# Batch 0's last expert as a slot of 7 + 7 products, its weights made in spaced steps through batch 0

## The chip, the cores and the metric

One NeuronCore of a Trainium2 chip runs the whole program. The metric is the device time of one execution in microseconds (us). Five engines work side by side, each through its own queue in program order: TensorE (PE; its weight loads are PEld), VectorE (DVE), ScalarE (ACT), GpSimd (POOL) and SyncE (SP), which issues nearly all DMA transfers. An instruction at the head of a queue that waits holds everything behind it in that queue.

## The reference, cut to what matters

```python
def reference(q, k, v, centroids, w_gate, w1, w2):      # 4 batches, 8 heads, 768 tokens, head dim 64
    x = clustered_attention(q, k, v, centroids)         # tokens x 512, all batches in one: 3072 x 512
    P = exp(x @ w_gate - max); 8 rounds of row and column normalizing    # 3072 x 8
    out = 0
    for e in range(8):                                  # 8 experts, w1[e] 512 x 1024, w2[e] 1024 x 512
        h = maximum(x @ w1[e], 0)
        out += P[:, e:e+1] * (h @ w2[e])
```

Everything is float32. The kernel keeps each float32 factor as a pair of float16 numbers (high and low) and adds three matmuls, so a product of blocks is 3 matmuls for every 128 of the inner dimension.

## The kernel before, in words

The attention comes first (about 490 us). The experts follow: batch 0 in one way, batches 1 to 3 in another.

**Layer 1** (`layer1`, with `product`) is the same everywhere. For a quarter of an expert's hidden features (256 of 1024, `f2`) it computes h = x w1 by a 2 x 2 block scheme with seven products instead of eight. A product is six matmuls of 128 x 384. Order of the seven: B11 into the accumulator `pa`; S2 x T2 into `pb`; then A12 onto `pa`, S3 onto `pb`, S1 into a new `pa`, A22 onto `pb`, S4 onto the second `pa`. ACT copies the first one (`m1`, L1379) and the third (L1617). DVE reads the others in L1370: `u2` after product 1, `u3` after 3, then the results called `c` after products 4, 5 and 6. `h_ps` has two buffers. So the `pb` of the next quarter's second product takes the buffer that DVE's last `c` of this quarter reads.

**Batch 0** runs 32 quarters (t = 0 to 31: expert t // 4, quarter t % 4). Step m = 0 to 6 of quarter t holds one product of layer 1 and, for m > 0, one token tile of the layer 2 of quarter t - 1 (`layer2`): six matmuls of 128 x 512 into `o_ps`, all eight block products. In between stand, written out by hand and kept in that order on every engine by `plan.keep_order`, the steps of generators:

- `make_w`: while quarter t runs, the float16 pairs of the weights of quarter t + 1 are made from `raw` (a float32 load, 8 buffers): ACT scales (L1482), POOL forms four sums (`s1w`, L336) and the low halves (L1487, L1494), ACT the high halves, DVE the low halves of the second matrix (`wb`, L1472, two instructions).
- `scan`: two ACT instructions per quarter (`total`, L302) measure the size of the weights of a later quarter (t + 5); after an expert's fourth quarter `spread_powers` turns the figure into the expert's scale. It is a chain over two DMAs: DVE `am` (L1456), DMA `amw` to memory, DMA `all` back to every partition, seven small DVE instructions that begin with `gmax` (L1302) and end with `so` (L273). An expert's fourth scan stands in quarters t = 6, 10, 14, 18, 22 and 26. The scan's generator advances at m in `ANY`, five times per quarter.
- `next_x`: from t = 9 on the same kind of chain for the inputs of batch 1 (`amx`).
- `store_w`: SP writes the made weights to memory for the later batches (`w1d`, `w2d`: four DMAs per quarter).
- `layer2`'s `done`: in quarters t % 4 == 0 the finished expert is added to `acc` by DVE (L1555, six instructions of 128 x 512); expert 0's is copied by ACT (L1552) and later gated (`gate_first`, L1564).

`second_left` makes, at the end of batch 0, the sums of w2 of expert 0 that the seven-product layer 2 needs.

**Batches 1 to 3** run 24 slots, one per batch and expert. A slot has 28 steps: one product of layer 1 (L1356) and nine matmuls of 128 x 256 of the layer 2 of the slot before (`layer2b`, L1814: seven products, 252 matmuls), with the weights loaded as made. In the first slot layer 1 stands alone. `evict` (L1789) adds finished products to the four blocks C11, C12, C21, C22 and X. During batch 1 the sums of w2 of experts 1 to 7 are made (`second_sums` and what follows it).

## Time and profile before

| | |
|---|---|
| median of 3 runs | 2289.27 us (2289.05 to 2291.24) |
| the profiled execution's own time | 2289.5 us |
| its span, first to last instruction | 2287.7 us |
| PE busy | 2257.7 us, 99% |
| DVE busy | 1637.3 us, 72% |
| POOL busy | 1145.9 us, 50% |
| ACT busy | 1113.2 us, 49% |
| mean granted clock of TensorE | 0.998 |
| share of PE in the chain that ended last | 92% |

The span is what the trace sees; the execution's own time has 1.8 us more around it. "Busy" of PE is pipelined: one matmul's shown duration overlaps the next one's, so the pace of PE is read from the distance of starts. A quarter's place in time is read from the starts of its first product, and T below is that start.

### The profile page before, as it was taken

The numbers are of one execution on the slowest core, as the hardware profiler recorded it, in microseconds if no ns is written. First come the engines' busy times: TensorE is split into PE (matmuls) and PEld (weight loads), VectorE is DVE, ScalarE is ACT, GpSimd is POOL, SyncE is SP. The second block draws the span as 40 slices with busy tenths as digits, with TensorE's granted clock in tenths as the row PEclk, the third lists the DMA queues.
The fourth block names the chain that finished last, engine by engine and source line by source line (L and its number), as shares of the span: only waits on it lengthen the run. The fifth ranks groups of instructions, "written<-read, shape, count | busy, mean of one in ns | idle before, by whom it ended". The sixth has DMA issues, their size and how long they took to land.

```text
span 2287.7 us, 39676 instructions
## 1 busy us (share of the span) xinstructions
PE 2257.7 (99%) x15491; PEld 1523.3 (67%) x15491; DVE 1637.3 (72%) x2691; ACT 1113.2 (49%) x2048; POOL 1145.9 (50%) x1009
## 2 busy tenths in 40 slices
...
GB/s 173 120 125 162 168 157 159 118 167 239 196 150 170 195 158 131 221 262 212 211 233 219 226 222 177 169 128 152 151 159 137 187 169 133 129 132 137 143 116 102
DMA packets 226828, 383.93 MB, mean 168 GB/s; under 512 B 73408, under 2 KB 154640, under 8 KB 226128
## 3 DMA queue, kind: packets, MB, share of 16 engines
...
q14 instruction: 67, 0.55, 0.1%
...
## 4 chain that ended last, share of the span: by engine, by line
PE 92%; DVE 3%; DMA 2%; ACT 1%; POOL 1%; issue 1%; SPq 0%; ACTq 0%; DVEq 0%; POOLq 0%
PE h_ps L1356 37%; PE pb L1814 12%; PE pc L1814 8%; PE pa L1814 8%; PE av_ps L978 5%; PE o_ps L1540 3%; PE o_ps L1542 3%; PE o_ps L1541 3%; PE max_ps L835 3%; PE exp_ps L923 3%; PE exp_ps L924 2%; PE misc_ps L636 1%; PE misc_ps L1020 1%; POOL psum L945 1%; DVE mrt L839 1%
## 5 line engine op out<-in xcount | busy, mean ns | idle before, releaser
L1356 PEld LDWEIGHTS <-wa 128*128 128x128 f16 x5376 | 525.7, 98 | 300.0 <-issue 2.1
L1814 PEld LDWEIGHTS <-ho 128*128 128x128 f16 x6048 | 591.4, 98 | 139.7 <-DVE ho L1708 2.5
L1356 PE MATMUL h_ps<-xsT,wa 128*128 128x384 f16 x3072 | 581.6, 326 | 0.3 <-DVE u L1370 0.2
L1699 POOL TENSOR_TENSOR B<-B,B 128x768 f32<-128x768 f32 x96 | 196.5, 2049 | 488.2 <-DVE ho L1708 468.0
L1356 PE MATMUL h_ps<-xsB,wa 128*128 128x384 f16 x2304 | 436.7, 326 | 0.3 <-ACT m L1379 0.3
L1708 DVE TENSOR_TENSOR ho<-B,ho 128x768 f16<-128x768 f32 x288 | 350.2, 1217 | 0.1
L1370 DVE SCALAR_TENSOR_TENSOR u<-h_ps,m 128x384 f32<-128x384 f32 x256 | 141.7, 554 | 271.1 <-PE h_ps L1356 267.0
L1854 ACT ACTIVATE B<-B 128x384 f32<-128x384 f32 x288 | 149.7, 520 | 378.8 <-DVE B L1370 375.4
L1814 PE MATMUL pb<-w2o,ho 128*128 128x256 f16 x2592 | 328.7, 273 | 0.4 <-DVE ho L1708 0.4
L1704 ACT CAST ho<-B 128x768 f16<-128x768 f32 x288 | 230.3, 825 | 11.2 <-POOL B L1699 7.8
L839 DVE TENSOR_REDUCE mrt<-max_ps 128x1 f32<-128x512 f32 (+1 forms) x288 | 190.5, 685 | 54.3 <-PE max_ps L835 52.7
L945 POOL TENSOR_TENSOR psum<-psum,pe 128x512 f32<-128x512 f32 x160 | 208.0, 1318 | 35.0 <-ACT pe L930 28.1
L1814 PE MATMUL pa<-w2o,ho 128*128 128x256 f16 x1728 | 219.2, 273 | 1.2 <-DVE ho L1708 1.2
L1814 PE MATMUL pc<-w2o,ho 128*128 128x256 f16 x1728 | 219.2, 273 | 0.2 <-DVE ho L1708 0.2
L1699 POOL TENSOR_TENSOR B<-B,T 128x768 f32<-128x768 f32 x48 | 94.6, 1973 | 230.0 <-DVE ho L1708 207.7
L930 ACT ACTIVATE pe<-exp_ps 128x512 f32<-128x512 f32 x288 | 166.9, 598 | 51.2 <-PE exp_ps L924 39.5
L1379 ACT ACTIVATE m<-h_ps 128x384 f32<-128x384 f32 x128 | 62.6, 489 | 191.0 <-PE h_ps L1356 187.2
L1852 ACT ACTIVATE B<-h_ps 128x384 f32<-128x384 f32 x96 | 47.1, 490 | 203.3 <-PE h_ps L1356 203.3
L1542 PE MATMUL o_ps<-wb,hl 128*128 128x512 f16 x384 | 145.5, 379 | 0.0
L1541 PE MATMUL o_ps<-wb,hh 128*128 128x512 f16 x384 | 145.5, 379 | 0.0
L1540 PE MATMUL o_ps<-wb,hh 128*128 128x512 f16 x384 | 145.5, 379 | 0.0
L1370 DVE SCALAR_TENSOR_TENSOR B<-h_ps,u 128x384 f32<-128x384 f32 x192 | 105.9, 552 | 48.3 <-PE h_ps L1356 48.2
...
## 6 DMA issues: line engine op xcount, KB each, us to landing
...
```

The source lines that it names most:

```text
L839: nc.vector.tensor_reduce(out=t["mr"][:, i0 : i0 + ni, ni - 1], in_=ps.rearrange("p (x c) -> p x c", x=ni), axis=AX, op=ALU.max)
L930: nc.scalar.activation(pe, ps.rearrange("p (x c) -> p x c", x=ni), AF.Exp, scale=SCALE)
L945: (nc.gpsimd if e == POOL else nc.vector).tensor_tensor(out=st[:, o : o + N0], in0=old[o], in1=part, op=ALU.add)
L1356: nc.tensor.matmul(ps[:, 0:HB], wa[:, w_, a, c, :], x[:, x_, c, :], start=(first and s_ == 0), stop=(s_ == len(steps) - 1), skip_group_che ...
L1370: nc.vector.scalar_tensor_tensor(out=t, in0=ps[:, 0:HB], scalar=KAPPA, in1=x, op0=ALU.mult, op1=ALU.add)
L1540: nc.tensor.matmul(po[i], hh[:, t, ti], wbh[:, t], start=(first and t == 0), stop=False)
L1541: nc.tensor.matmul(po[i], hh[:, t, ti], wbl[:, t], start=False, stop=False)
L1542: nc.tensor.matmul(po[i], hl[:, t, ti], wbh[:, t], start=False, stop=(last and t == 1))
L1699: nc.gpsimd.tensor_tensor(out=t, in0=d[a], in1=d[c], op=ALU.subtract)
L1704: nc.scalar.copy(t[:, 0], blocks[n, g][o])
L1708: nc.vector.tensor_tensor(out=t[:, 1], in0=blocks[n, g][o], in1=t[:, 0], op=ALU.subtract)
L1814: nc.tensor.matmul(ps[:, q], h[:, h_, f, q * P : (q + 1) * P], w[:, 2 * g + f, w_], start=(first and g == 0 and s_ == 0 and q % 2 == 0), s ...
```

## The change

Batch 0 runs 28 quarters (`N1`) instead of 32. Its expert 7 becomes the first slot, ahead of those of batch 1: layer 1 alone in that slot, layer 2 by seven products in the next. The four blocks C11 to C22 are what batch 0 adds into (in place of `acc`), and stay for the slot; `done` writes 128 x 256 twice where it wrote 128 x 512 once, and the outputs leave from the slot.

The weights of expert 7 are made in batch 0 by steps ("chores") at fixed places: a step stands at the end of step m of quarter t where 7 t + m is its number. `last_scan` loads each of the eight halves (256 KB) and lets ACT measure it in place (t = 3 to 7); `last_scale` forms the scale (t = 7 to 9); `last_first` and `last_second` load each quarter of each matrix again and make it, one of four quarters of the expert every four quarters from t = 9 to t = 26. Their buffers take 15 KB per partition; `raw` has 7 buffers instead of 8 and loads six quarters ahead instead of seven. Expert 0's sums of w2 are made in batch 1 like those of 1 to 6, and `second_left` is gone. In quarters t % 4 == 2 the scan's generator advances at all seven steps, not five.

The diff, cut to its core:

```diff
-        rawp = pool("rawp", 8, ax)
-        accp = pool("accp", 1, ax)
+        rawp = pool("rawp", 7, ax)
+        lastp = pool("lastp", 1, ax)
...
-        def second_left(f2):
...
+        chores = {}
+
+        def spaced(gen, first, offsets):
+            for o in offsets:
+                chores.setdefault(first + o, []).append(gen)
+
+        def load_last(m, f2):
+            t = lastp.tile([P, 1024], F32, name="lr", bufs=2)
...
+        def last_first(f2):
+            raw = load_last(0, f2)
...
+            yield
+            nc.scalar.activation(raw, raw, AF.Copy, scale=s1[:, E - 1 : E])
+            yield
...
+            quads = ((slice(A22, A22 + 1), A[:, 0, 1:2]), (slice(A11, A12 + 1), A[:, 1]))
+            for o, a in quads:
+                nc.scalar.copy(y[:, 0, o], a)
+            sums(S_, A[:, 1, 0], A[:, 1, 1], A[:, 0, 0], A[:, 0, 1], nc.gpsimd)
+            yield
+            for o, a in quads:
+                nc.gpsimd.tensor_tensor(out=y[:, 1, o], in0=a, in1=y[:, 0, o], op=ALU.subtract)
+            yield
+            nc.sync.dma_start(out=d[:, :, A22 : A12 + 1], in_=y)
+            yield
+            y = raw.bitcast(F16).rearrange("p (x o c f) -> p x o c f", x=2, o=4, c=KC)
+            nc.scalar.copy(y[:, 0], S_)
+            yield
+            for o in (0, 2):
+                nc.gpsimd.tensor_tensor(out=y[:, 1, o : o + 2], in0=S_[:, o : o + 2], in1=y[:, 0, o : o + 2], op=ALU.subtract)
+            yield
+            nc.sync.dma_start(out=d[:, :, S1 : S4 + 1], in_=y)
+            yield
+
+        FIRST_AT = (1, 7, 12, 13, 16, 19, 20, 24)
+
+        def last_second(f2):
+            raw = load_last(1, f2)
...
+            for o, a in quads:
+                nc.scalar.activation(y[:, o, 0], a, AF.Copy, scale=scale)
+            yield
+            for o, a in quads:
+                nc.vector.scalar_tensor_tensor(out=y[:, o, 1], in0=a, scalar=scale, in1=y[:, o, 0], op0=ALU.mult, op1=ALU.subtract)
+            yield
...
+            sums(S_, r2[:, 1, 0:HD], r2[:, 0, 0:HD], r2[:, 1, HD:DO], r2[:, 0, HD:DO], nc.gpsimd)
...
+        SECOND_AT = (1, 7, 10, 12, 14, 19, 22, 25)
+
+        def last_scan(f2, m, am):
+            t = load_last(m, f2)
+            yield
+            total(am[:, m, f2 : f2 + 1], t, t)
+            yield
...
+        for f2 in range(NP2):
+            for m in range(2):
+                spaced(last_scan(f2, m, am_last), 7 * (3 + f2), (1 + 3 * m, 7 + 3 * m))
+            spaced(last_first(f2), 7 * (3 + 6 + 4 * f2), FIRST_AT)
+            spaced(last_second(f2), 7 * (3 + 8 + 4 * f2), SECOND_AT)
+        spaced(last_scale(am_last), 7 * (3 + 4), (5, 8, 11, 14))
...
-                    nc.vector.scalar_tensor_tensor(out=acc[:, i], in0=ps, scalar=gate, in1=acc[:, i], op0=ALU.mult, op1=ALU.add)
...
+                        else:
+                            nc.vector.scalar_tensor_tensor(out=t, in0=s_, scalar=gates_[:, i : i + 1], in1=t, op0=ALU.mult, op1=ALU.add)
...
-        AHEAD = 7
+        AHEAD = 6
...
-        for t in range(NI):
+        for t in range(N1):
...
-                if m in ANY:
+                if m in ANY or t % NP2 == 2:
                     step(scanning)
...
-                if t == NI - 1:
-                    step_left(m)
+                for x in chores.pop(7 * t + m, ()):
+                    step(x)
...
-    slots = [(b, e) for b in range(1, B) for e in range(E)]
+    slots = [(0, E - 1)] + [(b, e) for b in range(1, B) for e in range(E)]
...
-        if b == 1 and n:
+        if b == 1 and e < E - 1:
             first = base - SLOT
```

Where instructions moved, at three places. The first is DVE in quarter t = 6, the fourth quarter of the scan of expert 2 (t = 10, 14, 18 and 22 read alike). `gmax2` to `so` are the seven instructions that need the DMA `all2`; `c <- h_ps, u2` is the last result of the quarter. Before:

```order
L1370 SCALAR_TENSOR_TENSOR c_7297<-h_ps_7198,m1_7193 128x384
L1623 SCALAR_TENSOR_TENSOR hl_7185<-c_7277,hh_7184 128x384
L1472 SCALAR_TENSOR_TENSOR wb_7183<-raw_6539,s2_99,wb_7183 128x512
L1370 SCALAR_TENSOR_TENSOR c_7317<-h_ps_7270,u2_7205 128x384
L1623 SCALAR_TENSOR_TENSOR hl_7185<-c_7297,hh_7184 128x384
L1623 SCALAR_TENSOR_TENSOR hl_7185<-c_7317,hh_7184 128x384
L1302 TENSOR_REDUCE gmax2_7345<-all2_7301 128x2
L1303 TENSOR_SCALAR gmax2_7345<-gmax2_7345 128x2
```

After:

```order
L1370 SCALAR_TENSOR_TENSOR c_7335<-h_ps_7225,m1_7219 128x384
L1701 SCALAR_TENSOR_TENSOR hl_7211<-c_7312,hh_7210 128x384
L1302 TENSOR_REDUCE gmax2_7339<-all2_7293 128x2
L1303 TENSOR_SCALAR gmax2_7339<-gmax2_7339 128x2
L1304 TENSOR_SCALAR gmax2_7339<-gmax2_7339 128x2
L270 TENSOR_SCALAR ginv_7343<-gmax2_7339 128x2
L271 RECIPROCAL s1_98<-ginv_7343 128x1
L272 RECIPROCAL s2_99<-ginv_7343 128x1
L273 TENSOR_SCALAR so_100<-ginv_7343 128x1
L1476 SCALAR_TENSOR_TENSOR wb_7209<-raw_6546,s2_99,wb_7209 128x512
L1370 SCALAR_TENSOR_TENSOR c_7363<-h_ps_7305,u2_7232 128x384
```

The seven instructions moved from behind the quarter's last `c` and its two `hl` to a place ahead of the second `wb` and of that `c`.

The second is SP in the same quarter: the stores of the weights (`w1d5`, `w1d6` and their `w2d`), the pair `amw2`, `all2`, the loads `raw`, and after the change the loads `lr` of the chores. Before:

```order
L1529 DMA w1d5_109<-wa_6861 128x3584
L1531 DMA w2d1_6221<-wb_6862 128x2x256 x3
L1442 DMA raw_7179<-in_moe_w1 128x4x256
L1443 DMA raw_7179<-in_moe_w2 128x2x512
```

After, from the stores of quarter 5 on:

```order
L1607 DMA w1d5_109<-wa_6869 128x3584
L1609 DMA w2d1_6221<-wb_6870 128x2x256 x3
L1517 DMA lr_7163<-in_moe_w2 128x2x512
L1446 DMA raw_7205<-in_moe_w1 128x4x256
L1447 DMA raw_7205<-in_moe_w2 128x2x512
L1515 DMA lr_7253<-in_moe_w1 128x4x256
L1607 DMA w1d6_110<-wa_7045 128x3584
L1609 DMA w2d1_6221<-wb_7046 128x2x256 x3
L1295 DMA amw2_7270<-am2_7268 128x2
L1298 DMA all2_7293<-amw2_7270 128x256
L1517 DMA lr_7327<-in_moe_w2 128x2x512
```

A load `lr` stands ahead of quarter 6's stores; there are two `lr` buffers, so it waits until ACT has measured the one before the last.

The third is DVE in quarter t = 12, where expert 2 is finished (t = 16, 20 and 24 read alike): `acc` (after: C11 to C22) from `o_ps`. Before:

```order
L1370 SCALAR_TENSOR_TENSOR u3_8128<-h_ps_8074,m1_8069 128x384
L1623 SCALAR_TENSOR_TENSOR hl_8061<-c_8106,hh_8060 128x384
L1555 SCALAR_TENSOR_TENSOR acc_6310<-o_ps_7701,gates_8053,acc_6310 128x512
L1370 SCALAR_TENSOR_TENSOR c_8146<-h_ps_8139,u3_8128 128x384
L1472 SCALAR_TENSOR_TENSOR wb_8059<-raw_7179,s2_99,wb_8059 128x512
L1555 SCALAR_TENSOR_TENSOR acc_6310<-o_ps_7722,gates_8053,acc_6310 128x512
```

After:

```order
L1370 SCALAR_TENSOR_TENSOR u3_8214<-h_ps_8158,m1_8149 128x384
L1701 SCALAR_TENSOR_TENSOR hl_8141<-c_8191,hh_8140 128x384
L1636 SCALAR_TENSOR_TENSOR C11_6314<-o_ps_7764,gates_8133,C11_6314 128x256
L1636 SCALAR_TENSOR_TENSOR C21_6317<-o_ps_7764,gates_8133,C21_6317 128x256
L1567 SCALAR_TENSOR_TENSOR lq_8154<-lr_8031,s2_99,lq_8154 128x256 x3
L1370 SCALAR_TENSOR_TENSOR c_8237<-h_ps_8230,u3_8214 128x384
L1476 SCALAR_TENSOR_TENSOR wb_8139<-raw_7375,s2_99,wb_8139 128x512
L1636 SCALAR_TENSOR_TENSOR C22_6315<-o_ps_7785,gates_8133,C22_6315 128x256
L1636 SCALAR_TENSOR_TENSOR C12_6316<-o_ps_7785,gates_8133,C12_6316 128x256
```

Each addition became two, and three instructions of a chore stand ahead of the fifth product's `c`.

## Rows read from the trace of the kernel before

**Rows 1.** Busy time by stretch: columns us, PE, PEld, DVE, ACT, POOL (count), clock, DMA share, GB/s.

```profile
839.57:897.95 58.38, 58.38 (x313) 30.53 (x312) 39.66 (x62) 35.29 (x58) 31.36 (x32) 1.00 0.37 125
1156.71:1211.53 54.82, 54.82 (x423) 41.10 (x421) 48.16 (x68) 26.76 (x41) 34.64 (x25) 1.00 0.67 233
```

**Rows 2.** Timeline of PE, quarter 12: start us, us, instruction, count [idle before <-releaser].

```profile
664.09 1.14 PE L1356 MATMUL h_ps<-xsB,wa 128*128 128x384 f16 x6
...
678.68 1.14 PE L1356 MATMUL h_ps<-xsB,wa 128*128 128x384 f16 x6
679.66 1.14 PE L1356 MATMUL h_ps<-xsT,wa 128*128 128x384 f16 x6
```

**Rows 3.** Timeline of DVE, end of quarter 10 and into 11.

```profile
647.48 1.64 DVE L1472 SCALAR_TENSOR_TENSOR wb<-raw,s,wb 128x512 f16<-128x512 f32 x1
649.04 0.55 DVE L1370 SCALAR_TENSOR_TENSOR c<-h_ps,u 128x384 f32<-128x384 f32 x1
...
650.66 0.41 DVE L1302 TENSOR_REDUCE gmax<-all 128x2 f32<-128x256 f32 x1
...
651.97 0.55 DVE L1370 SCALAR_TENSOR_TENSOR u<-h_ps,m 128x384 f32<-128x384 f32 x1
```

**Rows 4.** Timeline of ACT, start of quarter 10.

```profile
636.46 1.05 ACT L302 ACTIVATE junk<-raw 128x1024 f16<-128x1024 f32 x1
...
637.50 1.14 ACT L1482 ACTIVATE raw<-raw,s 128x1024 f32<-128x1024 f32 x1
```

**Rows 5.** Timeline of SP's DMA issues, quarter 10.

```profile
642.96 0.33 SPq L1295 DMA_DIRECT2D amw<-am  x1
645.77 0.33 SPq L1298 DMA_DIRECT2D all<-amw  x1
```

**Rows 6.** Timeline of SP's DMA issues, quarters 13 and 14.

```profile
686.74 0.33 SPq L1295 DMA_DIRECT2D amx<-am  x1
687.13 0.43 SPq L1442 DMA_DIRECT2D raw<-in_moe_w  x1
...
695.37 0.34 SPq L1298 DMA_DIRECT2D all<-amx  x1
...
696.28 1.75 SPq L1531 DMA_DIRECT2D w2d<-wb  x3
701.34 0.33 SPq L1295 DMA_DIRECT2D amw<-am  x1
706.98 0.33 SPq L1298 DMA_DIRECT2D all<-amw  x1
```

**Rows 7.** Timeline of DVE, quarter 15.

```profile
711.82 0.42 DVE L1302 TENSOR_REDUCE gmax<-all 128x2 f32<-128x256 f32 x1 [2.70 <-DMA all<-amw]
```

**Rows 8.** Timeline of PE, quarter 15.

```profile
713.17 0.38 PE L1542 MATMUL o_ps<-wb,hl 128*128 128x512 f16 x1
713.74 1.14 PE L1356 MATMUL h_ps<-xsT,wa 128*128 128x384 f16 x6 [0.18 <-DVE u L1370]
```

**Rows 9.** Timeline of DVE, quarter 12.

```profile
673.52 0.74 DVE L1472 SCALAR_TENSOR_TENSOR wb<-raw,s,wb 128x512 f16<-128x512 f32 x1
674.35 0.75 DVE L1555 SCALAR_TENSOR_TENSOR acc<-o_ps,gates,acc 128x512 f32<-128x512 f32 x1
675.32 0.56 DVE L1370 SCALAR_TENSOR_TENSOR c<-h_ps,m 128x384 f32<-128x384 f32 x1 [0.22 <-PE h_ps L1356]
...
676.67 1.64 DVE L1472 SCALAR_TENSOR_TENSOR wb<-raw,s,wb 128x512 f16<-128x512 f32 x1
678.24 0.74 DVE L1555 SCALAR_TENSOR_TENSOR acc<-o_ps,gates,acc 128x512 f32<-128x512 f32 x1
678.90 0.54 DVE L1370 SCALAR_TENSOR_TENSOR c<-h_ps,u 128x384 f32<-128x384 f32 x1
```

**Rows 10.** Timeline of POOL, quarter 12.

```profile
675.18 2.59 POOL L1494 TENSOR_TENSOR wa<-s1w,wa 128x512 f16<-128x512 f32 x2 [2.11 <-ACT wa L1492]
```

**Rows 11.** The instructions of line L1789: count, min/median/max ns, first and last start, forms.

```profile
L1789 DVE SCALAR_TENSOR_TENSOR C<-pb,gates,C x195: 467/475/485, 1031.6 to 2238.3; 128x256 f32<-128x256 f32 x195
```

More of the change, by code (lines that the diff above doesn't have):

```diff
@@ L1508, in second_left @@
             sums(S_, r2[:, 1, 0:HD], r2[:, 0, 0:HD], r2[:, 1, HD:DO], r2[:, 0, HD:DO], nc.gpsimd)
             yield
-            y = t[:, 0:1024].bitcast(F16).rearrange("p (o x m) -> p o x m", o=4, x=2)
-            nc.scalar.activation(y[:, :, 0], S_, AF.Copy, scale=s2[:, 0:1])
+            nc.sync.dma_start(out=w2d[E - 1][:, A22 : A12 + 1, f2], in_=y)
             yield
-            nc.vector.scalar_tensor_tensor(out=y[:, :, 1], in0=S_, scalar=s2[:, 0:1], in1=y[:, :, 0], op0=ALU.mult, op1=ALU.subtract)
+            y = raw.bitcast(F16).rearrange("p (o x m) -> p o x m", o=4, x=2)
@@ L1514, in second_left @@
+            nc.scalar.activation(y[:, :, 0], S_, AF.Copy, scale=scale)
             yield
-            nc.sync.dma_start(out=w2d[0][:, 3:7, f2], in_=y)
+            nc.vector.scalar_tensor_tensor(out=y[:, :, 1], in0=S_, scalar=scale, in1=y[:, :, 0], op0=ALU.mult, op1=ALU.subtract)
             yield
-        LEFT_AT = ((0, 3, 4, 6), (1, 5, 6, 8), (2, 7, 8, 10), (3, 9, 10, 12))
-        def step_left(now):
-            for x, times in zip(lefting, LEFT_AT):
-                if now in times:
-                    step(x)
+            nc.sync.dma_start(out=w2d[E - 1][:, S1 : S4 + 1, f2], in_=y)
@@ new lines, in last_second, with last_scale @@
+            yield
[4 more added lines that the diff above has]
+            total(am[:, m, f2 : f2 + 1], t, t)
+            yield
+        def last_scale(am):
+            am2 = gs.tile([P, 2], F32, name="am2z", bufs=1)
+            nc.vector.tensor_reduce(out=am2, in_=am, axis=AX, op=ALU.max)
+            yield from spread_powers(am2, 2, f"amw{E - 1}", lambda g: weight_use(E - 1, g, gs))
+        am_last = gs.tile([P, 2, NP2], F32, name="am8z", bufs=1)
@@ L1563, in gate_first @@
             for i in range(NT):
-                nc.scalar.activation(acc[:, i], acc[:, i], AF.Copy, scale=gates_[:, i : i + 1])
+                j, q_ = divmod(i, NT // 2)
+                for name, (r, j_) in PARTS.items():
+                    if j_ == j:
+                        t = acc[name][:, q_]
+                        nc.scalar.activation(t, t, AF.Copy, scale=gates_[:, i : i + 1])
                 yield
-        AHEAD = 7
+        AHEAD = 6
         RIDES = ((0, 6), (1, 1)) + tuple((t, m) for t in (2, 3, 4, 5) for m in (2, 6))
@@ L1579, in attn_moe_kernel @@
         plan.unpin()
-        acc = accp.tile([P, NT, DO], F32, name="acc")
-        lefting = []
+        acc = {name: accb.tile([P, NT // 2, HD], F32, name=name) for name in PARTS}
         gating = iter(())
-        scans = {i - 5: (i,) for i in range(8, NI)}
-        loads = {0: (), 1: (4, 5), 2: (6, 7, 8), 3: (9, 10)}
+        scans = {i - 5: (i,) for i in range(8, N1)}
+        loads = {0: (), 1: (4, 5), 2: (6, 7, 8), 3: (9,)}
         loaded = {}
-        for t in range(NI):
+        for t in range(N1):
             e, f2 = divmod(t, NP2)
```

70 lines of the change are left out of this document (41 added, 29 removed).

## The prediction

> **What bounds the kernel now.** I looked first at the shares of busy time: PE is busy for 99% of the span at a granted clock of 0.998, so a change pays only by taking matmuls away, and costs only where it makes PE wait. Then the busy time by stretch: an expert of batch 0 in steady state (quarters 24 to 27) takes 58.38 us of PE with 313 matmul records, a slot of the later batches 54.82 us with 423 [rows 1]. PE is full in both, so the two lengths are the prices of the two ways to do an expert.
>
> Then the timelines of a quarter, to see how near the other engines are to making PE wait. PE starts quarter 12 at 664.09 and quarter 13 at 678.68, and the second product of quarter 13 at 679.66 [rows 2]: a quarter is 14.59 us, and its successor's second product stands at T + 15.57 (T = the quarter's start). That product writes the buffer which DVE's last `c` reads. So **the last `c` has to end by T + 15.57**, or PE waits. In quarter 10 (T = 634.90, two quarters before the start in rows 2) it ends at 649.04 + 0.55 = 649.59, T + 14.7; in quarter 12 at 678.90 + 0.54 = 679.44, T + 15.35 [rows 3, 9]. There the slack is 0.22 us, and quarters 16, 20 and 24 read alike. Batch 0 is full on PE and nearly full on DVE around one instruction per quarter.
>
> **What the change takes away.** Four quarters of batch 0 become one slot: 58.38 - 54.82 = **-3.56 us** [rows 1]. By the order, 144 matmuls of 128 x 512 go and 252 of 128 x 256 come, which is that exchange. The drain of the last quarter, the lone layer 1 of the first slot and all of the attention stay. The gain is certain as long as the new slot is fed: its loads and seven-product steps are those of the other slots.
>
> **The scale chain in quarters 10, 18 and 22.** The seven instructions from `gmax` to `so` wait for the DMA `all`. Before, they stood behind the last `c`: in quarter 10 `gmax` starts at 650.66 and the next `u` at 651.97, so the block is 1.31 us [rows 3], and nothing urgent stood behind it. Now it stands ahead of the second `wb` and the last `c`. When does `all` land? Before, SP issued `amw` at 642.96 (T + 8.06) and `all` at 645.77, 2.81 later [rows 5]; an `all` issued at 706.98 released DVE at 711.82, 4.84 later [rows 6, 7]. The scan now takes seven steps, so `amw` comes after ACT's `total` (1.05), scale (1.14), the other `total` and one chore: from 636.46 (T + 1.56) on [rows 4], about T + 1.6 + 3.4 = T + 5.0. Then `all` is there at 5.0 + 2.81 + 4.84 = T + 12.65. DVE comes to the block at about that time. With 1.31 it ends at T + 14.0; the second `wb` takes 0.74 to 1.64 [rows 9, 3] and `c` 0.55: T + 15.3 to 16.2 against 15.57, so 0 to 0.65 lost. Each 0.1 us that `all` comes later is 0.1 more. Taken 0.5 each, bounds 0 to 1.5: **+1.5** for three.
>
> **Quarter 14.** Here two chains share SP. `amx` is issued at 686.74 and raw loads right behind it at 687.13; its successor `all` can be issued only at 695.37, 8.63 later, where the pair of quarter 10 took 2.81 [rows 6, 5]. SP waits at that instruction. Behind it stand the stores of quarter 14 (`w2d` at 696.28) and, behind these, `amw` at 701.34, `all` at 706.98 [rows 6]. DVE gets it at 711.82 after 2.70 us of idleness [rows 7]. Quarter 15 starts at 707.87 and so before this cost PE almost nothing: 713.74 - 713.17 = 0.57 between two starts whose pace is 0.22, so 0.35 [rows 8]. After the change the same block stands ahead of quarter 14's last `c`, whose bound is 693.28 + 15.57 = 708.85. If SP's queue is as before, `gmax` starts at 711.82; with 1.31, a `wb` of 0.74 and `c` of 0.55, `c` ends at 714.4: 5.5 us late. The earlier scan does not help, since `amw` waits behind the stores and not for ACT. Less the 0.35 that goes: **+5.2**. The lower bound is 0.1 (0.5 like the other quarters, if `amx` lands as fast as a lone `amw`).
>
> A page of the Trainium skill speaks against this: "DMA: Bandwidth & Descriptors", section "Anatomy of one DMA — SWDGE (gpsimd) path", gives a DMA a fixed cost of about 2.0 us plus its bytes at 436 GB/s. For a DMA of another queue type than these, so it is an estimate here: `amw` 2.0 and `all` (128 x 256 float32, 131 KB) 2.3, together 4.3 us. The rows show 2.81 + 4.84 = 7.65, and 8.63 for a few bytes ahead of large loads [rows 5 to 7].
>
> **Quarter 6.** It has the same block, and the loads `lr` of the first scan. A load `lr` stands ahead of quarter 6's stores and waits for ACT to have measured an earlier buffer. ACT's first three instructions of a quarter reach from T + 1.56 to about T + 3.7 [rows 4], and behind the wait SP has stores (1.75 for three issues [rows 6]) before `amw`: `amw` at T + 6.5 or later, `all` at T + 14.1 to 16.9. `c` then ends at T + 16.7 to 19.5, or 1.1 to 3.9 late. Taken **+2.0**, bounds 0 to 4.
>
> **Quarters 12, 16, 20 and 24.** Each addition to `acc` of 0.75 [rows 9] becomes two of 128 x 256; the slots' additions of that shape take 0.475 [rows 11], so +0.2 each. Three chore instructions of that shape stand ahead of the fifth product's `c`: 3 x 0.48 = 1.4. Of this the idle 0.22 ahead of the `c` at 675.32 hides a part, and DVE's order of work lets some be made up later. The slack at the end is 0.22. Sharing is a second cost: the `wb` that runs while POOL makes `wa` (675.18 to 677.77) takes 1.64, the one just before 0.74 [rows 9, 10], and the chores bring more POOL work to these quarters. A quarter loses between 0 and 1.4 + 0.2 + 0.9 - 0.22 - 0.22 + 0.2, about 1.9. Taken 0.5: **+2.0** for four, bounds 0 to 7.6.
>
> **Nothing** for the rest: the chores' loads (16 of 256 KB for the scan and the making, in 24 quarters) go beside a DMA share of 0.37 [rows 1]; `raw` with 7 buffers and 6 quarters ahead is still loaded some 80 us early; ACT is busy for 35.3 and POOL for 31.4 of 58.4 us [rows 1], so their added steps find room, except where said. At the seam the new slot's lone layer 1 needs no new weights in time that SP didn't store quarters before. If the x tiles of batch 1 are reloaded late there, 0 to 2.7 us, one quarter's slack of the other terms; taken 0.
>
> **The sum**: -3.56 + 1.5 + 5.2 + 2.0 + 2.0 = +7.1 on the profiled execution's 2289.5, which is 2296.6. The median of the runs is 0.2 below the profiled execution: **2296.4 us**.
>
> **The rivals.** *E, the contention at each chore quarter.* The same as the forecast, but quarters 12 to 24 lose their 1.9 each and quarters 10, 18, 22 1.0 each: 2296.4 + 5.6 + 1.5 = 2303. For it: 0.22 us of slack, and a `wb` at 1.64 wherever POOL writes. Against: DVE is busy only 39.7 of 58.4 us [rows 1]. It decides as soon as the chores' POOL sums fall beside the second `wb`.
>
> *B, not slower: the two queues on SP don't meet.* In the changed kernel the raw loads have other places (six ahead instead of seven), so `amx` may land as fast as a lone `amw`. Then quarter 14 costs its lower bound of 0.1, the block waits little (0.2 in each of quarters 10, 18 and 22, 1.0 in quarter 6) and quarters 12 to 24 lose 0.25 each: -3.56 + 0.1 + 0.6 + 1.0 + 1.0 = -0.9, so 2288.4. For it: what I see beside the 8.63 is the load right behind `amx`, and the loads moved. Against: some load still follows. A part of this case is that the pair `amw`, `all` is faster than the rows of quarter 10 show: issued at T + 5.0, a pair of 4.3 us would be there at T + 9.3, ahead of DVE, and quarters 10, 14, 18 and 22 would lose nothing. With quarter 6 at its 2.0 and quarters 12 to 24 at 0.25 each that is -3.56 + 2.0 + 1.0 = -0.6, 2288.7. The 4.3 us is what the page of the Trainium skill named under quarter 14 would give by its prices; the rows speak for 7.65.
>
> *D, everything hidden.* All stalls at nothing, and the 0.35 of quarter 15 and some 0.2 elsewhere recovered: 2289.3 - 3.56 - 0.55 = 2285.2. For it: every lower bound above is near 0. Against: four independent places would have to hold with slacks of 0.2 us. The matmul count offers nothing more, so much under 2285 is not to be had.
>
> *That the change doesn't do what it says* is excluded by the order: the 144 and the 252 matmuls are there.
>
> **How the numbers follow.** A measurement of this kernel tells 0.2% (4.6 us) from no change: faster is below 2284.7, slower above 2293.9. The forecast has 0.50, with a range of its own of 2293 to 2300 (0.05 of it below 2293.9); E 0.15; B 0.21; D 0.14, of which 0.04 falls below 2284.7. Faster 0.04; same 0.05 + 0.21 + 0.10 = 0.36; slower 0.45 + 0.15 = 0.60. Of B's chance, 0.06 is the fast pair that the Trainium skill's page would give. The range 2286.5 to 2303 leaves out about half of E (0.08) and most of D (0.12).
>
> **What would show it.** Right: in the profile after, PE gaps in nine quarters (6, 10, 12, 14, 16, 18, 20, 22, 24), each ended by DVE's last `c`, at quarter 14 the largest at 4 to 6 us with DVE idle for `all`; the seam without gaps; the first slot 54.8 us long. The step on quarter 14 is wrong if the `all` behind `amx` is issued within 4 us of it, or if `amw` stands ahead of the stores. The step on quarters 12 to 24 is wrong if `c` ends before T + 15.57 there. A gap that ACT or a load ends (a chore that holds up `m1`, expert 7's weights late at the seam) is a cost I didn't price and would make the forecast too low; a time under 2290 means that the moved block never waits for its DMA.

## The result and the profile after

The changed kernel takes **2309.55 us** (median of 6, 2307.53 to 2311.63), the kernel before 2288.91 in the same comparison (6 runs): a ratio of 1.0091, 95% interval 1.0078 to 1.0104. It is 20.6 us slower; forecast were 2296.4 with a range up to 2303.0. The direction was right, the size was not, and the time lies outside the range.

The windows of both kernels from the start of quarter 0 to the end, first before, then after (columns: us, then PE, PEld, DVE, ACT, POOL busy with counts, clock, DMA share, GB/s), show where the time is:

```profile
491.72:2287.68 1795.96, 1788.57 (x12631) 1233.08 (x12628) 1282.80 (x2034) 801.44 (x1324) 785.72 (x580) 1.00 0.53 174
```

```profile
490.48:2308.06 1817.58, 1790.47 (x12739) 1244.82 (x12736) 1308.19 (x2093) 809.05 (x1354) 807.65 (x588) 1.00 0.53 178
```

The stretch is 21.62 us longer; PE has 108 instructions more, as the order said (144 less, 252 more). The mean granted clock rounds to 1.00 in both, but after the change it fell twice for a few us, which is shown below. The attention ahead of it, which the change leaves alone, began quarter 0 at 491.72 and 490.48; over all profiled kernels of this study that point lies between 488.2 and 493.1. Medians therefore carry a spread of some 2 us, and the experiments below are read by this stretch and by the lengths of the quarters first, by the medians second.

Who makes PE wait at layer 1's line (engine and line that waits, who ended it; us in total, times, the longest), before and after:

```profile
PE h_ps L1356 <- DVE u L1370: 0.2, 1, 0.2
```

```profile
PE h_ps L1356 <- DVE c L1370: 20.4, 10, 5.5
```

Before, that was the wait of [rows 8] alone. After, it is DVE's `c`, as forecast. The waits are not all of the loss. PE's two longest, 5.52 and 4.34 us, are those behind quarters 6 and 14, and there the granted clock of TensorE fell to 0.50, which is 1.2 GHz in place of 2.4: during the first wait, and 0.79 us after the end of the second. The windows of the lowered clock (columns as above), then PE's product after the second wait (the one after the first stands under quarter 6):

```profile
595.33:602.16 6.83, 5.13 (x15) 2.14 (x15) 3.19 (x9) 4.81 (x9) 0.21 (x1) 0.50 0.88 321
725.03:728.44 3.41, 3.41 (x11) 1.36 (x9) 1.74 (x8) 2.17 (x4) 1.08 (x2) 0.50 1.03 397
```

```profile
724.24 1.34 PE L1356 MATMUL h_ps<-xsT,wa 128*128 128x384 f16 x6 [4.34 <-DVE c L1370]
```

The second product of the next quarter starts 5.68 and 4.51 us late in these two places, and the quarters become 8.19 and 6.18 us longer. So **4.2 us of the loss (2.51 + 1.67) is matmuls at half the clock after a long wait**, not waiting. In the other quarters the second product is 1.85 us late at most, the clock stays at 1.00, and the loss is the lateness.

The lengths of the quarters, as differences of the starts of their first products, give each loss, wait and clock together. In the table a loss stands at the quarter whose last `c` is late; it is the next quarter's length less 14.60 us (less 14.87 for quarter 5's). Where the block stands behind the last `c` (before, e1, e2, e10), the losses at quarters 6 and 14 are waits for the next quarter's `u` instead, as in [rows 8]. The last four columns are experiments told below.

| quarter | before | after | slot alone (e2) | move alone (e3) | chores alone (e1) | four repairs (e10) |
|---|---|---|---|---|---|---|
| 4 and 5 | 0 | 0.49 | 0 | 0 | 0.49 | 0.49 |
| 6 | 0 | 8.19 | 0 | 0.81 | 0.86 | 0 |
| 10 | 0 | 1.58 | 0 | 0.08 | 0 | 0 |
| 12 | 0 | 1.84 | 0 | 0 | 1.85 | 0 |
| 14 | 0.34 | 6.18 | 0.91 | 6.93 | 0.44 | 0.23 |
| 16 | 0 | 1.84 | 0 | 0 | 1.85 | 0 |
| 18 | 0 | 1.67 | 0 | 0.75 | 0 | 0 |
| 20 | 0 | 1.84 | 0 | 0 | 1.99 | 0 |
| 22 | 0 | 1.67 | 0 | 0.76 | 0 | 0 |
| 24 | 0 | 0.97 | 0 | 0 | 0.97 | 0.16 |
| sum | 0.34 | 26.27 | 0.91 | 9.33 | 8.45 | 0.88 |
| the stretch less the sum | 1795.62 | 1791.31 | 1791.28 | 1791.32 | 1792.52 | 1791.36 |

(e1's quarter 0 is 1.18 us longer than that of the others, 11.46 against 10.28; with that off, its last line is 1791.34. e1 and e10 also lose 0.09 at quarter 19, which is not counted.) All these kernels with the slot agree within 0.1 us once their losses are off. So **the exchange is worth 4.3 us** (1795.62 - 1791.3), the losses are all in these quarters, and the seam has none.

**Quarter 6.** SP's issues (start us, us):

```profile
579.74 0.37 SPq L1515 DMA_DIRECT2D lr<-in_moe_w  x1
580.20 0.45 SPq L1607 DMA_DIRECT2D w1d<-wa  x1
580.75 3.43 SPq L1609 DMA_DIRECT2D w2d<-wb  x3
584.27 0.44 SPq L1295 DMA_DIRECT2D amw<-am  x1
589.37 0.33 SPq L1298 DMA_DIRECT2D all<-amw  x1
```

And DVE, then PE:

```profile
588.63 0.54 DVE L1701 SCALAR_TENSOR_TENSOR hl<-c,hh 128x384 f16<-128x384 f32 x1
594.45 0.42 DVE L1302 TENSOR_REDUCE gmax<-all 128x2 f32<-128x256 f32 x1 [5.27 <-DMA all<-amw]
...
596.43 0.55 DVE L1370 SCALAR_TENSOR_TENSOR c<-h_ps,u 128x384 f32<-128x384 f32 x1
```

```profile
597.03 2.08 PE L1356 MATMUL h_ps<-xsT,wa 128*128 128x384 f16 x6 [5.52 <-DVE c L1370]
```

T is 575.44. The load `lr` leaves at T + 4.3, when ACT has measured the buffer; the stores follow, and `amw` at T + 8.83. It then takes 5.10 us to the issue of `all` (589.37) and `all` another 5.08 to DVE's start: T + 19.0. In quarter 10 of the kernel before the first of these was 2.81 [rows 5]. The row of PE at 2.08 us is a product at clock 0.50; at 1.00 it is 1.14 [rows 2].

**Quarter 18** (22 alike): here `all` is there in time, and the block itself is slow. DVE, then POOL:

```profile
783.19 0.68 DVE L1303 TENSOR_SCALAR gmax<-gmax 128x2 f32<-128x2 f32 x1
783.90 1.08 DVE L1304 TENSOR_SCALAR gmax<-gmax 128x2 int32<-128x2 int32 x1
785.02 1.08 DVE L270 TENSOR_SCALAR ginv<-gmax 128x2 f32<-128x2 f32 x1
786.13 0.16 DVE L271 RECIPROCAL s<-ginv 128x1 f32<-128x1 f32 x1
...
787.23 0.55 DVE L1370 SCALAR_TENSOR_TENSOR c<-h_ps,u 128x384 f32<-128x384 f32 x1
```

```profile
781.25 2.60 POOL L1491 TENSOR_TENSOR wa<-raw,wa 128x256 f16<-128x256 f32 x2
783.80 2.27 POOL L1498 TENSOR_TENSOR wa<-s1w,wa 128x512 f16<-128x512 f32 x2
786.03 0.72 POOL L336 TENSOR_TENSOR ls<-lr 128x256 f32<-128x256 f32 x1
```

An instruction on two numbers for each partition, 0.17 us in quarter 6, takes 0.68 to 1.08: each ends 0.02 to 0.03 us after a POOL instruction does (taken singly, the first `wa` of 783.80 ends at 784.96, the 1.08 of L1304 at 784.98). The reciprocals keep their 0.14 to 0.16.

Quarter 10 has some of both: DVE waits there for `all`, and two of the small instructions take 0.57 and 0.63, so the block is 2.27 us long, against 3.72 in quarters 18 and 22.

```profile
655.88 0.42 DVE L1302 TENSOR_REDUCE gmax<-all 128x2 f32<-128x256 f32 x1 [0.64 <-DMA all<-amw]
```

### The profile page after: what moved, and what is told of

It reads as the page before. It is cut to its first block, busy times and chain, and to the rows that moved or that the text cites. A ratio compares the mean times of both kernels' runs of the same rounds, so it can differ in the third digit from the quotient of the medians.

```text
span 2308.1 us, 39997 instructions
## 1 busy us (share of the span) xinstructions
PE 2258.6 (98%) x15599; PEld 1533.9 (66%) x15599; DVE 1663.0 (72%) x2750; ACT 1121.4 (49%) x2078; POOL 1167.9 (51%) x1017
## 4 chain that ended last, share of the span: by engine, by line
PE 86%; DVE 5%; DMA 3%; ACT 3%; POOL 1%; issue 1%; SPq 1%; DVEq 0%; ACTq 0%; POOLq 0%
PE h_ps L1356 35%; PE pb L1890 12%; PE pc L1890 8%; PE pa L1890 8%; PE av_ps L978 5%; PE max_ps L835 3%; PE exp_ps L923 3%; PE exp_ps L924 2%; PE o_ps L1618 2%; PE o_ps L1620 2%; PE o_ps L1619 2%; PE misc_ps L636 1%; PE misc_ps L1020 1%; DVE wb L1476 1%; DMA amw<-am 1%
## 5 line engine op out<-in xcount | busy, mean ns | idle before, releaser
L1890 PEld LDWEIGHTS <-ho 128*128 128x128 f16 x6300 | 616.1, 98 | 145.6 <-DVE ho L1784 2.5
L1775 POOL TENSOR_TENSOR B<-B,B 128x768 f32<-128x768 f32 x100 | 206.4, 2066 | 513.7 <-DVE ho L1784 496.0
L1784 DVE TENSOR_TENSOR ho<-B,ho 128x768 f16<-128x768 f32 x300 | 365.7, 1220 | 0.1
L1890 PE MATMUL pb<-w2o,ho 128*128 128x256 f16 x2700 | 342.5, 273 | 0.4 <-DVE ho L1784 0.4
L1780 ACT CAST ho<-B 128x768 f16<-128x768 f32 x300 | 239.9, 824 | 12.1 <-POOL B L1775 8.6
L1890 PE MATMUL pa<-w2o,ho 128*128 128x256 f16 x1800 | 228.4, 273 | 1.2 <-DVE ho L1784 1.2
L1890 PE MATMUL pc<-w2o,ho 128*128 128x256 f16 x1800 | 228.4, 273 | 0.2 <-DVE ho L1784 0.2
L978 PE MATMUL av_ps<-pe,vn 128*64 128x512 f32 (+1 forms) x768 | 134.2, 492 | 0.0
L1620 PE MATMUL o_ps<-wb,hl 128*128 128x512 f16 x336 | 128.4, 382 | 0.0
L1619 PE MATMUL o_ps<-wb,hh 128*128 128x512 f16 x336 | 128.3, 382 | 0.0
```

The source lines that it names most:

```text
L978: nc.tensor.matmul(av[o, a:z], vn[:, i, :], heads[t]["pe", c][:, i - i0], start=(i == 0), stop=False, skip_group_check=True)
L1619: nc.tensor.matmul(po[i], hh[:, t, ti], wbl[:, t], start=False, stop=False)
L1620: nc.tensor.matmul(po[i], hl[:, t, ti], wbh[:, t], start=False, stop=(last and t == 1))
L1775: nc.gpsimd.tensor_tensor(out=t, in0=d[a], in1=d[c], op=ALU.subtract)
L1780: nc.scalar.copy(t[:, 0], blocks[n, g][o])
L1784: nc.vector.tensor_tensor(out=t[:, 1], in0=blocks[n, g][o], in1=t[:, 0], op=ALU.subtract)
```

## Experiments

### The block and the chores, each alone

e1 undoes the move of the block; e2 leaves only the slot; e3 is the move without the chores.

```diff
# e1 (and e2)
-                if m in ANY or t % NP2 == 2:
+                if m in ANY:
# e2 and e3: of last_first and last_second only the stores stay
-            raw = load_last(0, f2)
...
-            nc.sync.dma_start(out=d[:, :, A22 : A12 + 1], in_=y)
+            nc.sync.dma_start(out=d[:, :, A22 : A12 + 1], in_=lq_.rearrange("p (x a c f) -> p x a c f", x=2, a=3, c=KC))
```

> The changed kernel with one part undone: in quarters 2, 6, 10, ... the scan advances at five steps again, so the seven instructions from gmax to so stand behind the quarter's last c. All chores stay. Theory A (the moved block makes the losses of quarters 6, 10, 14, 18 and 22, which are 8.2, 1.6, 6.2, 1.7 and 1.7 us by the starts of the quarters; the DVE chores make those of 12, 16, 20 and 24, 1.8, 1.8, 1.8 and 1.0): most of 19.4 us goes, with some 3 left at quarter 6 and 1.5 at quarter 14 because all still lands late there: 2309.5 - 19.4 + 4.5 = 2294.6 (2290 to 2298). The losses after quarters 12, 16, 20, 24 stay as they are. Rival R (the chores' loads on SP and their sharing with POOL cost the same wherever the block stands): 2304 or more.

> The exchange alone: 28 quarters and the new slot, the scan at five steps, and of the chores only the stores (of a constant tile; the loads, scaling, sums, halves, measuring and the scale of expert 7 are left out, so expert 7's part of batches 0 to 3 is missing from the output). Theory A: the exchange is worth the 3.6 us of the two stretches plus at most 0.5: 2285.2 (2284.3 to 2286.3). Rival R2 (the exchange itself gains less than the stretches say, for instance because the new first slot or the seam waits): 2287 to 2290.

> As the run of the exchange alone (stores of a constant tile only), with the scan at all seven steps in quarters 2, 6, 10, ...: the block ahead of the last c, but without chores. Theory A: quarter 14 loses its 6.2 us as in the changed kernel, because amw stands behind the loads there with or without chores; quarters 10, 18 and 22 lose little (0 to 0.5 each) since POOL has no chore left beside the block; quarter 6 loses 0 to 1.5 without a load ahead of the stores: 2285.2 + 6.2 + 0.7 + 0.8 = 2292.9 (2291 to 2295). Rival (the move costs only together with the chores): 2285 to 2287. Rival (the move costs all of it alone): 2304.

Measured: e1 2294.46 us (ratio to before 1.0026, 1.0015 to 1.0036), e2 2284.76 (0.9985, 0.9976 to 0.9994), e3 2293.39 (1.0017, 1.0007 to 1.0026). All three medians lie inside theory A's ranges, and the table shows that its places are right; of the sizes, e1's rests at quarters 6 and 14 (0.86 and 0.44, expected 3 and 1.5) and e3's losses at quarters 18 and 22 (0.75 and 0.76, expected 0.5 at most) were off. e2 and e3 leave out expert 7's weights, so their results lack its part. Quarters 12, 16, 20 and 24 belong to the chores alone. Quarter 14 belongs to the move alone. Quarter 6 belongs to neither: 0.81 and 0.86 apart, 8.19 together. Quarters 18 and 22 have half from the move and half from both. The sums 9.33 and 8.45 don't make 26.27; some 9 us is interaction, and it is the part that no single look at either edit gives. At quarter 6, 2.5 us of it is the clock, which falls only in the run with both edits; of e3's 6.93 at quarter 14, 2.4 is the clock.

### Quarter 14: which step holds SP

```diff
# e4: load_raw(t + AHEAD) of t = 14 after its fifth step
+                if t == 14 and m == 4:
+                    load_raw(t + AHEAD)
# e5: the same maximum in two columns
-        am = gs.tile([P, 1], F32, name="am")
-        nc.vector.tensor_reduce(out=am, in_=am4, axis=AX, op=ALU.max)
+        n = 2 if b == 1 else 1
+        am = gs.tile([P, n], F32, name=f"am{n}x")
+        for i in range(n):
+            nc.vector.tensor_reduce(out=am[:, i : i + 1], in_=am4, axis=AX, op=ALU.max)
```

> The changed kernel with one load moved: quarter 14's two raw loads are issued after its fifth step, so that on SP they no longer stand between amx and its all. Theory A (the loads behind amx make it land late; SP waits for it, and the stores, amw and the block wait behind): amx lands in about 3 us instead of 7.7, amw is issued at about T + 5, and the loss at quarter 14 falls from 6.2 to that of quarter 10, 1.6: 2309.5 - 4.6 = 2304.9 (2303.5 to 2306). Rival (amx lands late for another reason, or amw waits for the stores' traffic): no change, 2308 to 2310.5.

> The changed kernel with amx of batch 1 written as 128 x 2 (8 bytes for a partition, like amw; both columns alike) in place of 128 x 1. With the raw loads out of its way amx still landed 7.4 us after its issue, so the loads are not what holds it. Theory S (the 4-byte writes themselves land late; amw, with 8, lands in 2.8 to 3.5): amx lands in 3 to 4 us, all is issued by then, the stores and amw follow earlier, and the loss at quarter 14 falls from 6.2 to 1.6 to 2.5: about 2305 (2304 to 2306.5). Rival P (what holds it is its place, in quarter 13): amx takes over 7 us again, 2308 to 2310.5.

SP's issues in the changed kernel, in e4 and in e5:

```profile
697.79 0.33 SPq L1295 DMA_DIRECT2D amx<-am  x1
698.17 0.43 SPq L1446 DMA_DIRECT2D raw<-in_moe_w  x1
...
705.54 0.34 SPq L1298 DMA_DIRECT2D all<-amx  x1
...
709.16 0.33 SPq L1295 DMA_DIRECT2D amw<-am  x1
717.20 0.33 SPq L1298 DMA_DIRECT2D all<-amw  x1
```

```profile
696.56 0.33 SPq L1295 DMA_DIRECT2D amx<-am  x1
703.95 0.33 SPq L1298 DMA_DIRECT2D all<-amx  x1
...
708.03 0.44 SPq L1295 DMA_DIRECT2D amw<-am  x1
713.46 0.33 SPq L1298 DMA_DIRECT2D all<-amw  x1
```

```profile
697.36 0.33 SPq L1295 DMA_DIRECT2D amx<-am2x  x1
697.74 0.43 SPq L1448 DMA_DIRECT2D raw<-in_moe_w  x1
...
701.10 0.34 SPq L1298 DMA_DIRECT2D allx<-amx  x1
...
708.67 0.33 SPq L1295 DMA_DIRECT2D amw<-am  x1
712.61 0.33 SPq L1298 DMA_DIRECT2D all<-amw  x1
```

e4 took 2306.81 us and lost 4.42 at quarter 14 in place of 6.18 (2.88 late and 1.5 by the clock, where it was 4.51 and 1.7): 1.76 of the 4.6 us expected, and for another reason. Nothing stands behind `amx` any more, and its `all` still comes 7.39 later (7.75 in the changed kernel). The loads were not what held it; without them only `amw` lands sooner, 5.43 after its issue in place of 8.04. e5 took 2304.33 with the loads back in place: `all` comes 3.74 after `amx`, `amw` no longer stands behind stores issued just before it, the clock stays at 1.00, and the loss falls to 0.90. What was slow is **a write of 4 bytes for a partition** (512 bytes in all; the edit doubles both). In the same run the `amx` of batches 2 and 3, left at 4 bytes, landed 7.9 and 8.5 us after their issue by their completions in the trace.

### Quarter 6 and the chores on DVE

```diff
# e6: last_scan
-                spaced(last_scan(f2, m, am_last), 7 * (3 + f2), (1 + 3 * m, 7 + 3 * m))
+                spaced(last_scan(f2, m, am_last), 7 * (3 + f2), (2 + 2 * m, 7 + 3 * m))
# e7: last_second
-        SECOND_AT = (1, 7, 10, 12, 14, 19, 22, 25)
+        SECOND_AT = (1, 7, 8, 12, 14, 19, 22, 25)
```

> The changed kernel with last_scan's first load one step later in its quarter, so that on SP it stands behind the stores of the quarter and (in quarter 6) behind amw; all work stays. Theory A (in quarter 6 the load waits for ACT until T + 4.3 and holds the stores and amw behind it; amw then lands behind the stores' traffic): amw is issued at about T + 5.6 in place of T + 8.8, all lands at about T + 13.5 in place of T + 19.0, and the loss at quarter 6 falls from 8.2 to about 1: 2302.3 (2301 to 2304). Rival Q (ACT's crowding and the traffic make it, wherever the load stands): at most 2 us less, 2307.5 or more.

> The changed kernel with the three DVE instructions lq of last_second two steps earlier (quarters 12, 16, 20, 24, step 1 in place of 3), where DVE is idle for 1.4 us and POOL for 2.9. Theory A (at their old place they take 2.25 us, the second one 1.38 beside POOL's wa, and push the rest of the quarter's DVE work back): the losses of 1.8, 1.8, 1.8 and 1.0 fall to 0 to 0.3 each: 2303.4 (2302.3 to 2304.6). Rival T (the quarters are too full of DVE work wherever it stands, above all with the additions split in two): half or less is saved, 2306 or more.

e6 took 2302.43 us. SP in its quarter 6 (T = 574.00):

```profile
579.54 0.33 SPq L1295 DMA_DIRECT2D amw<-am  x1
579.96 0.39 SPq L1515 DMA_DIRECT2D lr<-in_moe_w  x1
583.21 0.33 SPq L1298 DMA_DIRECT2D all<-amw  x1
```

`amw` leaves at T + 5.54, `all` at T + 9.21, and the loss is 1.11 in place of 8.19, as expected; PE waits 1.1 us there and the clock stays at 1.00. (At quarter 14 this run loses 1.0 more than the changed kernel. 0.2 of it is a later `c`; 0.8 is the clock, which is at 0.50 for 6.83 us there in place of 3.41.)

e7 took 2305.19 us, 0.6 above the range expected, though quarters 12, 16 and 20 lose nothing and quarter 24 0.16 (the profiled run, 2302.59, lies inside it). Quarter 12 in the changed kernel, DVE and then POOL:

```profile
681.90 2.17 DVE L1567 SCALAR_TENSOR_TENSOR lq<-lr,s,lq 128x256 f16<-128x256 f32 x3
...
685.12 0.87 DVE L1636 SCALAR_TENSOR_TENSOR C<-o_ps,gates,C 128x256 f32<-128x256 f32 x2
...
687.61 1.64 DVE L1476 SCALAR_TENSOR_TENSOR wb<-raw,s,wb 128x512 f16<-128x512 f32 x1
...
689.16 0.86 DVE L1636 SCALAR_TENSOR_TENSOR C<-o_ps,gates,C 128x256 f32<-128x256 f32 x2
689.95 0.54 DVE L1370 SCALAR_TENSOR_TENSOR c<-h_ps,u 128x384 f32<-128x384 f32 x1
```

```profile
681.39 2.01 POOL L1491 TENSOR_TENSOR wa<-raw,wa 128x256 f16<-128x256 f32 x2
...
688.66 1.17 POOL L336 TENSOR_TENSOR ls<-lr 128x256 f32<-128x256 f32 x1
```

In e7 the same three instructions `lq`:

```profile
676.32 1.27 DVE L1567 SCALAR_TENSOR_TENSOR lq<-lr,s,lq 128x256 f16<-128x256 f32 x3
```

They cost 2.17 beside POOL's `wa` and 1.27 at a place where DVE had been idle and POOL began its next work 0.84 us later (677.16), and there they push nothing back. The additions in two halves, still in e7, are 0.86 to 0.88 for two against 0.75 for one [rows 9]; without the `lq` beside them the quarters take that up.

### What slows the moved block

```diff
-        FIRST_AT = (1, 7, 12, 13, 16, 19, 20, 24)
+        FIRST_AT = (1, 8, 12, 13, 16, 19, 20, 24)   # e8
+        FIRST_AT = (1, 8, 14, 15, 17, 19, 20, 24)   # e9
+        FIRST_AT = (1, 8, 16, 17, 18, 19, 20, 24)   # e11
```

> The changed kernel with ACT's scaling of the loaded quarter (last_first) one step later in quarters 10, 14, 18 and 22, behind the two measurings and the scaling of make_w. Theory A (this instruction puts make_w's scaling 0.9 us back on ACT, so POOL's sums and low halves come 0.9 us later and lie beside one more of the small DVE instructions of the moved block, which then take 1.08 in place of 0.17): the losses of quarters 10, 18 and 22 fall by 0.9 each, to those of the move alone (0.1, 0.8, 0.8), that of quarter 14 by 0 to 0.9: 2306.5 (2305.5 to 2307.5). Rival (the block's inflation is from the chores' own POOL work, the sums ls): no change.

> The changed kernel with two chores later in quarters 10, 14, 18 and 22: ACT's scaling behind make_w's (as in the run before with that name), and POOL's sums and low halves from the last two steps of the quarter to the first two of the next. In the run with ACT's scaling alone later, POOL went on with the sums right beside the moved block in quarters 18 and 22. Theory A (a small DVE instruction of the block waits for the POOL instruction that runs beside it, whichever it is): with both out of the way the losses of quarters 10, 18 and 22 fall from 1.6, 1.7 and 1.7 to those of the move alone, 0.1, 0.8 and 0.8: the stretch from quarter 0 to the end, 1817.6 us in the changed kernel, gets 3.3 shorter, and 1 more if quarter 6 varies as in that run. Rival (the chores cost there by DVE's own work, an lr instruction of 1.3 us early in the quarter): losses as before.

> The changed kernel with ACT's scaling chore behind make_w's and, in POOL's order, the sums ls and the low halves of last_first behind the next quarter's own POOL work (s1w, wa), which waits for ACT. In the run before, the sums stood ahead of that work in POOL's order, and as POOL was free they ran at the same time as ever, beside the block. Theory A (a small DVE instruction waits for the POOL instruction beside it): now POOL is idle when the last instructions of the block run; the losses of quarters 10, 18 and 22 fall from 1.6, 1.7 and 1.7 to 0.1, 0.8 and 0.8, and the stretch from quarter 0 to the end from 1817.6 to about 1814. New costs of up to 1 us in quarters 11, 15, 19 and 23 are possible, where the sums now lie. Rival (DVE's own chore work makes the difference to the move alone): quarters 18 and 22 still lose 1.6.

| | median, us | stretch | quarter 10 | quarter 18 | quarter 22 |
|---|---|---|---|---|---|
| changed kernel | 2309.55 | 1817.58 | 1.58 | 1.67 | 1.67 |
| e8 | 2310.24 | 1815.21 | 0.66 | 1.59 | 1.58 |
| e9 | 2307.87 | 1815.56 | 0.67 | 1.58 | 1.58 |
| e11 | 2315.00 | 1820.95 | 0.07 | 0.81 | 0.82 |

(e8's stretch and quarters are from its profiled run, 2305.20 us, the fastest of four and 5 below the median. Quarter 10 lost 0.89 to 0.91 in e4, e5 and e6 too, where nothing there was edited, so its 0.66 says little.)

e8 and e9 missed. In quarter 18 of both, make_w's POOL work comes 0.9 us earlier as meant, and POOL then goes on with the sums `ls` at 14.57 after the quarter's start, beside the block. In e9 the sums stand a step later in the order, but POOL was free and their inputs were there, so they ran as before: a later place in the order of an idle engine moved nothing. In e11 they stand behind work that waits for ACT. POOL and DVE in quarter 18 of e11:

```profile
782.77 2.58 POOL L1498 TENSOR_TENSOR wa<-s1w,wa 128x512 f16<-128x512 f32 x2
791.05 0.73 POOL L336 TENSOR_TENSOR s1w<-raw 128x256 f32<-128x256 f32 x1 [5.69 <-issue]
```

```profile
784.30 1.08 DVE L1304 TENSOR_SCALAR gmax<-gmax 128x2 int32<-128x2 int32 x1
785.42 0.17 DVE L270 TENSOR_SCALAR ginv<-gmax 128x2 f32<-128x2 f32 x1
```

With POOL idle, `ginv` takes 0.17 where it took 1.08, and the losses are those of the move alone (0.08, 0.75, 0.76), as theory A said. L1304 still runs beside POOL's `wa`, and still takes 1.08. The time as a whole was missed: the sums now lie in quarters 11, 15, 19 and 23, of which three lose 0.5 to 2.2, and quarters 12, 16, 20 and 24 lose 2.3 to 2.7 in place of 1.0 to 1.8. I didn't follow that further.

The Trainium skill, "SBUF — State Buffer", section "Who interferes with whom", gives the rule for this: DVE shares a pair of SBUF ports with GpSimd; an operation like `tensor_scalar` can take both ports and then has the pair for itself or waits for it, "the other fully blocks"; one with at most one SBUF input, outside these modes, doesn't contend. The traces agree on both sides: 0.17 against 1.08 for `gmax` and `ginv`, and the additions from PSUM (one SBUF input) at 0.43 a piece beside POOL's `ls` (the rows at 689.16 and 688.66).

### A version without the losses

e10 has all the chores and the slot with four repairs: e1's scan, e5's write, e6's load, e7's place.

> All chores and the slot, with four repairs at once: the scan at five steps again, amx with 8 bytes for a partition, last_scan's first load behind the stores, and lq two steps earlier. Theory A (the three causes are additive and independent of each other once the block stands behind the last c): the losses sum to 0.2 to 1.2 in place of 26, and the kernel comes to the exchange alone: from the run with the scan back, 2294.5 less 5.7 (quarters 12, 16, 20), 0.8 (24), 0.6 (6) and 0.4 (14), less the 1.2 by which its profiled start was late, if the runs share that: 2286 (2284.3 to 2287.5), against 2288.6 for the kernel before. Rival (something of the chores stays, for instance ACT crowded in quarters 4 to 7 or the late lr loads): 2288 to 2291.

It took 2286.63 us (11 runs) against 2290.28 for the kernel before in that comparison (15 runs): ratio 0.9987, 0.9978 to 0.9995. The stretch (columns as above) and what PE still waits for DVE's `c` at this line:

```profile
490.89:2283.13 1792.24, 1785.26 (x12739) 1243.56 (x12736) 1305.82 (x2094) 808.63 (x1354) 808.53 (x588) 1.00 0.54 181
```

```profile
PE h_ps L1358 <- DVE c L1372: 0.2, 1, 0.2
```

It is within 0.1 us of the slot alone (1792.19) in this stretch with all weights made, its clock does not fall to 0.50 between quarter 0 and 2282 us, and it is faster than both kernels, by 0.13% than the one before.

## Why the prediction was right and wrong

| step | forecast | measured |
|---|---|---|
| the exchange | -3.56 | -4.3 |
| quarters 10, 18, 22 | +1.5 | +4.9 |
| quarter 14, net | +5.2 | +5.8 |
| quarter 6 | +2.0 | +8.2 |
| quarters 12, 16, 20, 24 | +2.0 | +6.5 |
| the rest | 0 | +0.5 |
| sum | +7.1 | +21.6 |

The 5.8 and the 8.2 hold 1.7 and 2.5 us of lowered clock. What failed is the sizes of three terms (quarter 6; 12 to 24; 10, 18 and 22), each taken near its lower bound, and that the clock was put at nothing.

**What bounds it: right.** All but 0.5 us of the losses are in the nine quarters that the prediction named, each ended by DVE's last `c` with the bound at T + 15.57, quarter 14 with DVE idle for `all`; the seam and the first slot have none.

**The clock was put at nothing, without a reason.** "Each 0.1 us that `all` comes later is 0.1 more" took the loss to be the lateness. That held for the short waits. Behind the two long ones the granted clock fell to 0.50, and the 10.2 us of lateness cost 14.4.

**The exchange** was under by 0.77: the two lengths of [rows 1] leave out the seam of the kernel before, whose first slot and its successor had 0.4 and 0.3 us more (quarters of 7.26 and 13.96 us where the new ones take 6.83 and 13.70), 0.69 in all, that is gone.

**Quarter 14** had the right size by luck, and the wrong cause. `gmax` did wait for a late `all`, but it started at T + 16.2 and not at T + 18.5, the block took 2.69 us and not 1.31, and `c` ended 4.5 us late and not 5.5; the clock added the 1.7 that make the sum fit:

```profile
720.38 0.42 DVE L1302 TENSOR_REDUCE gmax<-all 128x2 f32<-128x256 f32 x1 [3.32 <-DMA all<-amw]
723.64 0.55 DVE L1370 SCALAR_TENSOR_TENSOR c<-h_ps,u 128x384 f32<-128x384 f32 x1
```

I took the load right behind `amx` for the reason of the 8.63 us. e4 refutes that, e5 shows the 4 bytes. Nothing in the rows of before could tell the two apart, but the pair `amw`, `all` of quarter 10 differed from `amx` in two things, not one, and I named one. Rival B's condition for quarter 14 (the load moves away) was therefore worth 1.8 us, not 5.

**Quarter 6** is the largest miss, 6.2 us; 2.5 of it is the clock. The rest is the chain, and there the mechanism was the one described, a load that waits for ACT ahead of the stores and of `amw`. The mis-sized term was the way of `amw` itself: the bounds T + 14.1 and T + 16.9 have it at 2.81, from a quarter where SP had nothing else under way [rows 5], and at about the 5.64 of the same DMA behind stores [rows 6], and the +2.0 lies between the two, though stores stand ahead here. Measured were 5.10, and `amw` left at T + 8.8, not 6.5, because the third `w2d` was issued 1.7 us after the second. With 5.64 and 4.84 from T + 8.8 the sum would have been `all` at T + 19.3; it was there at T + 19.0, and `c` ended 5.6 late.

**Quarters 12 to 24** failed in the choice between the bounds: 0.5 had no row behind it. Three of the four lost 1.84, which is near the upper bound of 1.9, but not by its parts (and as written these add up to 2.26). The 0.9 for `wb` did not come: it takes 1.64 beside POOL's `wa` as it did before [rows 9]. The three instructions took 2.17 in place of 1.4, since the second of them ran beside POOL's `wa`. From quarter 12 before to after, the `c` behind them came 1.9 later against the quarter's start; idle time of DVE took up 0.35, an `hl` beside `wa` (1.31 for 0.95) and the next addition gave 0.5 back, and of the 2.0 the slack of 0.22 hid its part.

**Quarters 10, 18 and 22**: 1.31 us for the block was read where POOL was quiet [rows 3]. The place it moves to lies beside POOL's `wa`, which [rows 10] shows from T + 11.1 to 13.7, and there it takes 2.3 to 3.7. In quarters 18 and 22 `all` was in time, 3.73 and 3.80 after its issue, so the wait on which the step rested did not happen, and its cost did; quarter 10 waited 0.64. The pair took 6.6 and 6.9 us in quarters 18 and 22 and 8.5 in quarter 10, against 7.65 in the rows. The 4.3 us estimated from the Trainium skill's page ("DMA: Bandwidth & Descriptors", "Anatomy of one DMA — SWDGE (gpsimd) path") is below all three. Rival B was right that a pair faster than the rows' is there in time in two of the three, and wrong that the quarter then loses nothing.

**The rivals.** E had the right kind of cost for seven of the nine quarters at 2303 (its terms add up to 2303.5), with a chance of 0.15; what it lacked was quarter 6, whose 6.2 us more would have made it 2309.7. That this is so near is luck in part, since 4.2 us of the measured loss is a clock that no rival had. Most terms were taken near their lower ends and came out near or over their upper ones. They are not independent: the block and the three `lq` were priced as with POOL quiet, and `amw` nearly as with the queue quiet.

**Left open.** The loss at quarter 6 was 7.0 to 8.4 in the six other runs that have the changed kernel's code there: the second product was 5.0 to 5.8 us late and the clock took 1.6 to 2.7; why either varies is not shown. Nor is why a 4-byte write lands late: the trace has its packets done 1.0 us after the issue. The loads `lr` are 512 KB each by the trace, not the 256 KB of the forecast; what that is worth no run tells.
